# Attention, soft mixture of experts and a wide output layer: where the first two pairs' normalised values are computed, who issues the first loads of k, and another order of the attention's events

## The chip, the cores and the metric

One core of a Trainium2 chip runs the whole kernel as one program. The metric is the device time of one execution in microseconds (us). Engines are named as in the profile: PE (TensorE), DVE (VectorE), ACT (ScalarE), POOL (GpSimd) and SP (SyncE, which here only issues DMAs).

## The reference

q, k and v have the shape 4 x 12 x 448 x 64 (batch, heads, positions, columns). What is computed, cut to its core:

```python
q_n, k_n = rmsnorm(q, g_q), rmsnorm(k, g_k)        # x / sqrt(mean(x*x) + 1e-6) * g
scores = q_n @ k_n.T / sqrt(64)
attn = exp(scores - max) ; attn /= sum             # per row
x = (attn @ v), heads side by side                 # 1792 x 768
logits = x @ phi                                   # 768 x 32: 8 experts of 4 slots
slot_input = softmax(logits, axis 0).T @ x
slot_out[e] = relu(slot_input[e] @ w1[e]) @ w2[e]  # 768 x 1024 and 1024 x 768, 8 of each
x = softmax(logits, axis 1) @ slot_out
h = x @ w_in                                       # 768 x 2048
out = (max(h, 0) + alpha * min(h, 0)) @ w_out      # 2048 x 768
```

## The kernel before

**Tiles and stages.** The 48 heads are worked on as 24 pairs of two heads; two pairs that follow each other are a group and are loaded together. Each pair has 7 chunks of up to 128 rows (three per head and one that takes the rest of both heads). After the attention a soft mixture of experts follows (its statistics are gathered per batch, that is every six pairs), then eight experts whose weights stream in through eleven buffers of 1.5 MB, then the output layer. Seven of the eleven buffers lie where the attention's tiles were: two open when the last pair has been transposed and the event `cn` has come (`close_norm`), two at `cs` (the last scores), three at `ce` (the last products with v).

**The chain of a pair.** The loads of q and k (`load_to`, L599 to L612) bring a group into the tile qk. For each pair ACT squares it (sqr, L641; there is one buffer, `NSQ = 1`, L398) and DVE sums the squares into u (L643). For each group ACT and DVE turn u into the scale factors y (`norm_rs`, L653 to L663). `split_mul` (L668) makes the normalised values nf with three products: k times G, where G is the product of the two gains (L1151), then k times y, and q times y. There is one buffer nf (`"NNF": 1`). ACT casts nf to 16 bits (the high parts, L690), and `split_lo` (L692) subtracts them from nf to get the low parts (L697); both parts go into the tile sp. PE transposes sp (L710), ACT copies the result to the operands q and k (L717), and SP copies parts of these into the helpers qB and kB (L719, L721) and doubles q (L726).

The score rows are shifted by a coarse row maximum: PE computes the coarse scores (psr, L760), DVE reduces each to a maximum in the tile m (L769), PE turns m (L731), ACT copies it to mr (L737), and SP moves mr into a row of qB (L738). Then the scores proper are two matmuls a chunk, of k and q and of kB and qB (L778). ACT takes their exponential, once in 16 bits and once in 32 (L792 to L799), DVE or POOL subtract one from the other (L810), and PE multiplies with v (L827, L837). DVE also narrows the 64-bit weights w_in (win, L500 to L514) beside the attention.

**Who computes the products.** `T["PMUL"]` (L92) lists, for even and odd pairs, which of the three products (0 to 2) and two subtractions (3, 4) run on POOL. It lists all five for both, so POOL does all of them and DVE none.

**What sets the order.** The attention is written as 2374 small events (a product, a chunk's scores, one DMA piece, ...). Their order is the tuple `ORDER` (L232 to L350), a permutation worked out beforehand, and every engine executes its instructions in the order in which the events emit them; nothing is reordered later. Ahead of the events stand the constants, the loads of the first two groups of q and k, and the loads of the gains. All DMAs are issued by SP, one after the other.

Of the kernel before, what the change touches and what calls it, by code (L numbers as in the profile page):

```python
# [353 lines left out]
def fused_attention_softmoe_mlp(  # L354
# [15 lines left out]
    nc = tc.nc  # L370
    B, H, S, D = q.shape
# [6 lines left out]
    SM = 3 * P  # L378
# [213 lines left out]

    got = set()

    def load_to(g, src, dst, b0, t0):
        b, i = divmod(g * GP, NPAIR)
        s4 = src[b, 2 * i : 2 * (i + GP)].rearrange("(i h) t d -> h i t d", h=2)
        for h in range(2):
# [11 lines left out]
            ts = t0 + h if t0 == 6 else t0  # L610
# [414 lines left out]
    with tc.manual_schedule():  # L1025
# [120 lines left out]
        for _ in load_qk(0):  # L1146
            pass
# [403 lines left out]
```

## Time and profile before

| what | us |
|---|---|
| runs of the kernel before | 698.57, 696.68, 689.49 (median 696.68) |
| the profiled execution, its own time | 698.2 |
| its span, first to last instruction | 696.2 |

The span is what the rows below divide up; 2.0 us of the profiled execution lie around it. A group row gives the instructions of one line and tile with their mean duration, a stretch row the busy time of each engine in a piece of the span. In a timeline row the bracket gives how long the engine was idle before the instruction and who released it, as inferred.

### The profile page before, as it was taken

Reading aid. Unit: us, or ns where it says so; the run is one execution under the profiler, and the core shown is the slowest. Engines: PE = TensorE matmul, PEld = TensorE weight load, DVE = VectorE, ACT = ScalarE, POOL = GpSimd, SP = SyncE. Lnnn points to the kernel's source line nnn. Section 1 sums busy time; section 2 is a strip of 40 time slices with the busy share of each in tenths; the row PEclk is TensorE's granted clock in tenths of the full one; section 3 lists DMA queues with packets and bytes.
Section 4 is the critical chain, followed back from the end, with each engine's and each line's share of the span. In section 5 each row is a group of like instructions: output and inputs, shape, how many; then the busy total and the mean of one; then the engine's idle time right before and its main releaser. Section 6 shows DMA issues by size and latency. Waiting matters only on the chain.

```text
span 696.2 us, 14030 instructions
## 1 busy us (share of the span) xinstructions
PE 618.2 (89%) x5522; PEld 479.6 (69%) x5522; DVE 472.7 (68%) x967; ACT 364.5 (52%) x708; POOL 192.6 (28%) x200
## 2 busy tenths in 40 slices
PE   0799898898889999998998657899999999999997
PEld 0367665576656766775543213787899999999997
DVE  5788997899999999864311042999975545454541
ACT  2799996898898997772111121766531111111110
POOL 5976665466647654321101000000000000000000
PEclk9889999999999999998899979999999999999999
DMA  5477666644735622759799999250020101010101
GB/s 138 109 209 197 174 161 190 178 118 115 191 93 154 180 50 61 211 164 399 313 422 425 425 423 425 107 182 1 1 91 0 47 1 46 1 45 1 47 1 45
DMA packets 65425, 106.90 MB, mean 154 GB/s; under 512 B 34632, under 2 KB 51536, under 8 KB 61008
## 3 DMA queue, kind: packets, MB, share of 16 engines
q1 hardware_dynamic: 65360, 106.01, 45.6%
q8 instruction: 43, 0.70, 0.4%
q14 instruction: 22, 0.18, 0.1%
HBM read 92.18 MB, written 5.51 MB: 140 GB/s over the span
## 4 chain that ended last, share of the span: by engine, by line
PE 50%; DVE 23%; DMA 12%; ACT 8%; issue 3%; SPq 2%; POOL 2%; ACTq 0%; DVEq 0%; POOLq 0%
PE psa L1461 9%; PE psa L1460 9%; PE psa L1459 9%; DMA unit<-in_moe_w_dram 8%; DVE m L769 4%; PE psn L778 4%; PE psv L837 3%; PE psv L827 3%; PE psa L1285 2%; DVE e L810 2%; PE psr L760 2%; DVE wf L510 1%; ACT e L794 1%; PE psa L1314 1%; PE pst L1416 1%
## 5 line engine op out<-in xcount | busy, mean ns | idle before, releaser
L1459 PE MATMUL psa<-whi,gh 128*128 128x384 f32 (+1 forms) x448 | 152.7, 341 | 0.0
L1460 PE MATMUL psa<-wlo,gh 128*128 128x384 f32 (+1 forms) x448 | 151.8, 339 | 0.0
L1461 PE MATMUL psa<-whi,gl 128*128 128x384 f32 (+1 forms) x448 | 151.4, 338 | 0.0
L769 DVE TENSOR_REDUCE m<-psr 128x1 f16<-128x448 f32 x168 | 97.2, 615 | 5.9 <-PE psr L760 5.4
L1428 ACT CAST gh<-t 128x512 fp32r<-128x512 f32 x40 | 24.9, 622 | 123.0 <-DVE t L1425 122.5
L1461 PEld LDWEIGHTS psa<-whi,gl 128*128 128x128 f32 x448 | 84.7, 189 | 3.0 <-DVE gl L1408 0.2
L1460 PEld LDWEIGHTS psa<-wlo,gh 128*128 128x128 f32 x448 | 84.7, 189 | 2.8
L837 PE MATMUL psv<-vH,e 128*128 128x65 f16 (+1 forms) x1152 | 85.7, 195 | 1.0 <-DVE e L810 0.9
L1459 PEld LDWEIGHTS psa<-whi,gh 128*128 128x128 f32 x448 | 84.7, 189 | 2.6
L837 PEld LDWEIGHTS <-e 128*128 128x128 f16 (+1 forms) x1728 | 80.8, 106 | 1.5 <-DVE e L810 1.2
L1422 DVE TENSOR_SCALAR t<-pst,alpha_t 128x256 f32<-128x256 f32 x80 | 34.9, 476 | 61.9 <-PE pst L1416 61.9
L810 POOL TENSOR_TENSOR e<-ef,e 128x448 f16<-128x448 f32 x48 | 53.7, 1119 | 83.1 <-ACT ef L799 65.4
L827 PEld LDWEIGHTS psv<-vR,e 128*128 128x128 f32 (+1 forms) x384 | 59.6, 178 | 22.9 <-issue 10.9
L837 PE MATMUL psv<-vL,e 128*128 128x64 f16 (+1 forms) x576 | 73.7, 193 | 0.1
L794 ACT ACTIVATE e<-psn 128x448 f16<-128x448 f32 x120 | 65.1, 542 | 14.2 <-PE psn L778 11.1
L778 PE MATMUL psn<-q,k 128*128 128x448 f16 (+1 forms) x192 | 62.5, 368 | 11.0 <-DVE e L810 4.9
L827 PE MATMUL psv<-vR,e 128*128 128x65 f32 (+1 forms) x384 | 69.9, 264 | 1.9 <-DVE X L865 0.7
L760 PE MATMUL psr<-k,q 128*128 128x448 f16 (+1 forms) x192 | 58.8, 378 | 6.8 <-DVE m L769 4.0
L778 PE MATMUL psn<-qB,kB 67*128 67x448 f16 (+1 forms) x192 | 62.2, 364 | 2.8 <-DMA vR<-in_v_dram 2.8
L697 POOL TENSOR_TENSOR sp<-nf,sp 128x448 f16<-128x448 f32 x48 | 51.2, 1076 | 13.9 <-ACT sp L690 11.0
L810 DVE TENSOR_TENSOR e<-psn,e 128x448 f16<-128x448 f32 x72 | 44.2, 616 | 9.3 <-ACT psn L799 8.8
L710 PE MATMUL pst<-ident,sp 128*128 128x128 f16 x336 | 28.4, 233 | 19.2 <-POOL sp L697 19.0
(164 smaller groups left out, 1077.4 us busy)
## 6 DMA issues: line engine op xcount, KB each, us to landing
unit<-in_moe_w_dram SPq DMA_DIRECT2D x26, 1536.0 KB
unit<-in_moe_w_in_dram SPq DMA_DIRECT2D x24, 512.0 KB
rawo<-in_moe_w_out_dram SPq DMA_DIRECT2D x8, 1536.0 KB
unit<-in_moe_w_dram SPq DMA_DIRECT2D x36, 256.0 KB
out_dram<-osb SPq DMA_DIRECT2D x14, 384.0 KB
qk<-in_q_dram SPq DMA_DIRECT2D x24, 192.0 KB
qk<-in_k_dram SPq DMA_DIRECT2D x24, 192.0 KB
vR<-in_v_dram SPq DMA_DIRECT2D x48, 96.0 KB
```

Source lines behind the costliest of these rows:

```text
L697: eng.tensor_tensor(out=d["sp"][:, a, :, D:], in0=d["nf"][:, a], in1=d["sp"][:, a, :, 0:D], op=ALU.subtract)
L760: nc.tensor.matmul(pn[o0:o1, :S], d["q"][:, c0 : c0 + o1 - o0], d["k"][:, h * S : (h + 1) * S], start=True, stop=True)
L769: nc.vector.tensor_reduce(out=d["m"][:, c : c + 1], in_=d.pop(("pn", c))[:, :S], axis=AX.X, op=ALU.max)
L778: nc.tensor.matmul(pe[o0:o1, :S], lhs[:, c0 : c0 + o1 - o0], rhs[:, h * S : (h + 1) * S], start=st_, stop=not st_,)
L794: nc.scalar.activation(e2[:, 0], pe[:, :S], AF.Exp, scale=0.125)
L810: eng.tensor_tensor(out=e2[:, 1], in0=ef, in1=e2[:, 0], op=ALU.subtract)
L827: nc.tensor.matmul(pv[o0:o1, slot, :], d["e", c][:, qs], d["vv"][:, sl], start=(j == 0), stop=False,)
L837: nc.tensor.matmul(pv[o0:o1, slot, 0:wd], d["e", c][:, w // 2, qs], (vl if w == 1 else vh)[:, sl, 0:wd], start=(j == 0 and w == 0), stop=( ...
L1422: nc.vector.tensor_scalar(out=t0[:, cs], in0=ph[:, cs], scalar1=0.0, scalar2=alpha_t[:, f // 2, i : i + 1], op0=ALU.min, op1=ALU.mult)
L1459: nc.tensor.matmul(a, gh[f][:, ms], hi[:, hs], start=(f == 0 and not (packed and m % 2 == 1 and hf == 0)), stop=False)
L1460: nc.tensor.matmul(a, gh[f][:, ms], lo[:, hs], start=False, stop=False)
L1461: nc.tensor.matmul(a, gl[f][:, ms], hi[:, hs], start=False, stop=(f == KF - 1 and not (packed and m % 2 == 0 and hf == 1)))
```

## The change

Three things are changed. For pairs 0 and 1 the three products and two subtractions run on DVE instead of POOL. The four loads of k for the first group are issued by ACT instead of SP, and ACT's table load is placed behind them. The 2374 events of the attention are permuted anew.

```diff
 ORDER = (
-    1775, 968, 992, 1076, 920, 969, 993, 1016, 932, 1028, 1040, 1052, 1064, 1100, 1148, 1124, 921, 1796, 970, 994,
...
-    def load_to(g, src, dst, b0, t0):
+    def load_to(g, src, dst, b0, t0, eng=nc.sync):
...
-                    nc.sync.dma_start(
+                    eng.dma_start(
...
-            nc.sync.dma_start(dst[h * D : h * D + D, :, ts, :], s4[h, :, SM:S].rearrange("i p d -> p i d"))
+            eng.dma_start(dst[h * D : h * D + D, :, ts, :], s4[h, :, SM:S].rearrange("i p d -> p i d"))
...
         yield from load_to(g, q, qk[:, 0], 4, 3)
-        yield from load_to(g, k, qk[:, 1], 4, 3)
+        yield from load_to(g, k, qk[:, 1], 4, 3, nc.sync if g else nc.scalar)
...
-        eng = nc.gpsimd if w in T["PMUL"][n % 2] else nc.vector
+        eng = nc.gpsimd if n > 1 and w in T["PMUL"][n % 2] else nc.vector
...
-        eng = nc.gpsimd if 3 + a in T["PMUL"][n % 2] else nc.vector
+        eng = nc.gpsimd if n > 1 and 3 + a in T["PMUL"][n % 2] else nc.vector
...
-        nc.scalar.preload_act_table_set("natural_log_exp_and_others")
         for _ in load_qk(0):
             pass
+        nc.scalar.preload_act_table_set("natural_log_exp_and_others")
```

What the order does to the engines' lists is shown at three places. First ACT at the start, before (two squares for the first group, the y steps, the casts of pair 0, two squares for the next group, the copies of pair 0's transposes):

```order
L1145 ACT_TABLE_LOAD
L641 ACTIVATE sqr<-qk 128x896 x2
L653 ACTIVATE y<-u,eps 128x28
L654 ACTIVATE y<-y 128x28
L690 CAST sp<-nf 128x7x64
L641 ACTIVATE sqr<-qk 128x896
L690 CAST sp<-nf 128x7x64
L641 ACTIVATE sqr<-qk 128x896
L717 COPY q<-pst_230 128x896
L717 COPY k<-pst_257 128x896
L690 CAST sp<-nf 128x7x64
```

and in the changed kernel:

```order
L605 DMA qk<-in_k_dram 128x2x192
L611 DMA qk<-in_k_dram 64x2x64
L605 DMA qk<-in_k_dram 128x2x192
L611 DMA qk<-in_k_dram 64x2x64
L1147 ACT_TABLE_LOAD
L641 ACTIVATE sqr<-qk 128x896 x2
L653 ACTIVATE y<-u,eps 128x28
L654 ACTIVATE y<-y 128x28
L690 CAST sp<-nf 128x7x64 x2
L641 ACTIVATE sqr<-qk 128x896
L717 COPY q<-pst_236 128x896
L641 ACTIVATE sqr<-qk 128x896
```

The copy of k follows right behind. The second square of the next group stood ahead of both copies and now stands between them.

DVE at the same place, from its last constant on, before:

```order
L587 MEMSET X_134 128x128
L643 TENSOR_REDUCE u<-sqr 128x2x7 x2
L656 TENSOR_SCALAR u<-u 128x28
L659 TENSOR_TENSOR t<-y 128x28
L661 TENSOR_TENSOR t<-t,u 128x28
L663 SCALAR_TENSOR_TENSOR y<-t,y 128x28
L643 TENSOR_REDUCE u<-sqr 128x2x7 x2
L769 TENSOR_REDUCE m<-psr 128x1 x6
```

and in the changed kernel, from the last step of y on:

```order
L663 SCALAR_TENSOR_TENSOR y<-t,y 128x28
L684 TENSOR_TENSOR nf<-nf,y 128x448
L684 TENSOR_TENSOR nf<-qk,y 128x448
L697 TENSOR_TENSOR sp<-nf,sp 128x7x64 x2
L684 TENSOR_TENSOR nf<-qk,G 128x448
L684 TENSOR_TENSOR nf<-qk,y 128x448
L643 TENSOR_REDUCE u<-sqr 128x2x7
L684 TENSOR_TENSOR nf<-nf,y 128x448
L643 TENSOR_REDUCE u<-sqr 128x2x7
L769 TENSOR_REDUCE m<-psr 128x1
```

The products and subtractions of pair 0 stand ahead of the sums of the next group, and two products of pair 1 do too. (The first product of pair 0 stands between the two sums of the first group; the two subtractions of pair 1 come behind the first row maximum.)

SP around the maxima of pair 7 (mr into qB1; unit is an expert's or w_in's weight buffer, the numbers are those of tiles), before:

```order
L719 DMA kB2_119<-k_1664 64x896
L488 DMA unit_1493<-in_moe2_w_in_dram 128x1024
L726 DMA q_1438<-q_1438 64x896
L479 DMA unit_1760<-in_moe_w1_dram 128x512 x3
L738 DMA qB1_116<-mr_1778 1x7x128
L479 DMA unit_1760<-in_moe_w1_dram 128x512
L601 DMA vR0_122<-in_v_dram 128x3x64 x2
```

and in the changed kernel:

```order
L726 DMA q_1414<-q_1414 64x896
L488 DMA unit_1544<-in_moe2_w_in_dram 128x1024
L719 DMA kB2_119<-k_1712 64x896
L738 DMA qB1_116<-mr_1772 1x7x128
L479 DMA unit_1775<-in_moe_w1_dram 128x512 x2
L601 DMA vR0_122<-in_v_dram 128x3x64 x2
```

The three pieces of expert weights that stood ahead of the maxima now stand behind them. Of the three events that open weight buffers, `cn` stood behind the first four score chunks of pair 22 and now stands ahead of the first; `cs` stood behind the last products with v and now stands behind the last score chunk.

## Rows read from the trace of the kernel before

**Rows 1.** The page, busy us, share of the span and instructions of an engine.

```profile
PE 618.2 (89%) x5522; PEld 479.6 (69%) x5522; DVE 472.7 (68%) x967; ACT 364.5 (52%) x708; POOL 192.6 (28%) x200
```

**Rows 2.** Stretches: the attention proper and its last part (first line: the columns).

```profile
core 0: us, PE busy (x) PEld busy (x) DVE busy (x) ACT busy (x) POOL busy (x), PEclk, DMA share, GB/s
40.00:280.00 240.00, 217.39 (x2734) 159.78 (x2732) 225.37 (x463) 213.77 (x435) 145.19 (x136) 0.98 0.55 148
280.00:320.00 40.00, 39.40 (x573) 30.30 (x571) 27.84 (x70) 28.13 (x62) 11.15 (x11) 1.00 0.67 216
```

**Rows 3.** Stretches after the attention, columns as in rows 2.

```profile
336.00:338.00 2.00, 2.00 (x18) 0.55 (x12) 1.86 (x6) 0.00 (x0) 1.01 (x1) 0.87 0.02 4
...
400.00:420.00 20.00, 11.85 (x79) 3.68 (x80) 8.64 (x16) 4.51 (x6) 0.00 (x0) 0.74 1.01 423
...
480.00:696.00 216.00, 212.12 (x1229) 206.19 (x1227) 119.61 (x215) 48.80 (x84) 0.00 (x0) 1.00 0.07 26
```

**Rows 4.** Timeline of the start, and the experts' first matmul: start us, us, engine, line.

```profile
0.73 1.28 ACT L1145 ACT_TABLE_LOAD   x1 [0.73 <-PEq L1535]
...
3.32 0.60 SPq L605 DMA_DIRECT2D qk<-in_k_dram  x1
...
8.11 0.95 ACT L641 ACTIVATE sqr<-qk 128x896 f32<-128x896 f32 x1 [6.10 <-DMA gqk<-in_g_q_dram]
...
10.46 1.09 DVE L643 TENSOR_REDUCE u<-sqr 128x14 f32<-128x896 f32 x1
...
14.73 0.19 DVE L663 SCALAR_TENSOR_TENSOR y<-t,y 128x28 f32<-128x28 f32 x1
...
15.00 0.93 POOL L684 TENSOR_TENSOR nf<-qk,y 128x448 f32<-128x448 f32 x1 [2.16 <-DVE y L663]
...
16.79 2.16 POOL L697 TENSOR_TENSOR sp<-nf,sp 128x448 f16<-128x448 f32 x2
...
18.54 0.95 ACT L641 ACTIVATE sqr<-qk 128x896 f32<-128x896 f32 x1 [0.70 <-DVE u L643]
...
19.00 0.93 PE L710 MATMUL pst<-ident,sp 128*128 128x128 f16 x7 [0.20 <-POOL sp L697]
...
20.18 0.91 ACT L717 COPY k<-pst 128x896 f16<-128x896 f16 x1
...
21.91 2.02 POOL L697 TENSOR_TENSOR sp<-nf,sp 128x448 f16<-128x448 f32 x2
...
334.67 1.94 PE L1285 MATMUL psa<-unit,slT 128*32 128x512 f32 x8
```

**Rows 5.** Groups of DVE by shape: busy us, mean ns of one.

```profile
L1429 DVE TENSOR_TENSOR gl<-t,gh 128x512 fp32r<-128x512 f32 x40 | 27.5, 687 | 3.0 <-ACT gh L1428 2.3
...
L1252 DVE TENSOR_TENSOR wlo<-wf,whi 128x768 fp32r<-128x768 f32 x16 | 15.2, 952 | 1.0 <-ACT whi L1250 0.9
```

**Rows 6.** Tile vL on DVE (ns min/median/max), and DVE beside POOL at 42.7 us.

```profile
L747 DVE SCALAR_TENSOR_TENSOR vL<-vR,vH x24: 677/686/1510, 38.6 to 311.5; 128x512 f16<-128x512 f32 x24
...
42.73 1.31 DVE L747 SCALAR_TENSOR_TENSOR vL<-vR,vH 128x512 f16<-128x512 f32 x1
...
43.45 1.48 POOL L810 TENSOR_TENSOR e<-ef,e 128x448 f16<-128x448 f32 x1
```

**Rows 7.** Timeline around the scores of pair 7.

```profile
104.57 0.80 SPq L738 DMA_DIRECT2D qB<-mr  x1
...
111.11 0.46 PE L778 MATMUL psn<-qB,kB 67*128 67x448 f16 x1 [2.79 <-DMA vR<-in_v_dram]
...
113.77 0.63 DVE L769 TENSOR_REDUCE m<-psr 128x1 f16<-128x448 f32 x1 [1.52 <-PE psr L760]
...
116.17 0.62 DVE L810 TENSOR_TENSOR e<-psn,e 128x448 f16<-128x448 f32 x1 [1.77 <-ACT psn L799]
```

**Rows 8.** Stretches around the scores of pair 7, columns as in rows 2.

```profile
107.00:111.00 4.00, 0.90 (x11) 0.47 (x8) 3.85 (x9) 2.99 (x6) 4.00 (x4) 1.00 1.04 313
111.00:115.00 4.00, 3.89 (x39) 3.65 (x40) 1.88 (x4) 1.00 (x2) 2.52 (x4) 0.57 0.76 223
```

More of the change, by code (lines that the diff above doesn't have):

```diff
@@ L604, in load_to @@
             else:
-                nc.sync.dma_start(
+                eng.dma_start(
                     dst[:, :, b0 * h : b0 * h + 3, :].rearrange("p i r d -> p i (r d)"),
```

233 rows, old and new, of the table ORDER are left out of this document.

## The prediction

> **What bounds the kernel now.** I read the page's busy times first, then a table by stretches, then the stretches in which an engine that should be full is not. The page has PE at 89% and DVE at 68% of the span [rows 1], which are averages over stages with different limits. By stretches it looks otherwise. From 40 to 280 us, the attention proper, DVE is busy 225.37 of 240 us and PE 217.39, so DVE is the tighter one and idles only 14.6 us; from 280 to 320 us PE is, with 39.40 of 40 [rows 2]. After that the experts' weights bound: in 336 to 338 us the DMA queues move 4 GB/s, because every weight buffer is full and PE has only begun to use them, and from about 339 us on they move some 423 GB/s, to 420 us and beyond; in the last 216 us PE is busy 212.12 [rows 3]. The experts' first matmul starts at 334.67 [rows 4]. So the end of the attention is passed on one to one to the start of the experts, from there to the stream of weights and from there to the end, as long as the buffers are full when PE comes to them. The margin is that pause, some 4 us: an attention that is more than 4 us shorter would begin to wait for the weights instead. The code after the attention is not changed. What counts is when the attention begins at full pace, and how much DVE and PE idle in it.
>
> **The change part by part.** The loads of k for the first group go from SP's queue to ACT's. SP issued the first of them at 3.32 us, each takes 0.60 us of the queue, and the first square began at 8.11 us [rows 4]. Four issues, 2.6 us in all, now run beside SP's. But what a square feeds is the sum on DVE, and DVE is at its constants until that sum starts, without a wait, at 10.46 us, 1.4 us after the square had ended [rows 4]. DVE's list up to there is the same after the change, so earlier data only wait longer for DVE. ACT's table load, 1.28 us [rows 4], now stands behind the four issues and would end near 4.6 us, before any square. Should the constants end sooner than I think, at most the 2.4 us between 8.11 and 10.46 could be won; should k land later on the second queue, the square has 1.4 us to spare before anything is lost. I take 0.
>
> The second part is the ten products and subtractions of pairs 0 and 1. On POOL a product takes 0.93 us and two subtractions 2.16 [rows 4]. The trace has no such operation on DVE, so I bound it by two neighbours with both inputs in SBUF: 0.687 us for 512 columns and 0.952 for 768 [rows 5], which lie on a line that gives an estimate of 0.62 for 448 columns, and about 0.55 from one start to the next since they overlap by some 0.07. The scale factors y are ready at 14.92 us as before (the last step starts at 14.73) [rows 4]. Then, on DVE: product of k 14.95 to 15.57, of q to 16.1; ACT casts k 15.6 to 16.15 and q to 16.7; subtractions to 16.7 and 17.35. The transposes of q then run from 17.4 and those of k from 18.3 to 19.2, where the second set had begun at 19.00 and taken 0.93 [rows 4]: 0.7 us won. It is lost again on ACT. Before the change the second square of the next group stood ahead of both copies and ran at 18.54; the copy of k began at 20.18 [rows 4]. Now that square stands between the copy of q and the copy of k, and it needs the one square buffer that the sum on DVE frees, and this sum now stands behind two products of pair 1. That gives: products 17.35 to 18.45, sum to 19.5, square to 20.45, copy of k 20.45 to 21.35, against 20.18 to 21.09. For pair 1 the last subtraction comes out at 24.4 us by the same reckoning, against POOL's two that started at 21.91 and took 2.02 [rows 4]. The ten operations, 5.5 us of DVE, fall into time in which DVE waited. Sum of the front: 0, with 1.5 us to either side, as DVE's list from 21 to 37 us has a dozen small waits that I can't settle.
>
> Here a rule speaks against the change. In the trace DVE's subtraction for vL, median 686 ns, took 1.31 us at 42.73, and POOL's subtraction that began at 43.45 took 1.48, the two side by side [rows 6]. The Trainium skill (SBUF — State Buffer, Who interferes with whom) says that a DVE instruction with two SBUF inputs and a GpSimd instruction that reads SBUF exclude each other for a whole instruction; the trace agrees, with those 1.31 and 1.48 us. All ten moved operations have two SBUF inputs. They would meet POOL only if POOL worked beside them, and its next product, of pair 2, needs the single buffer nf, which pair 1 frees with the last of the ten. So I charge nothing, and keep the collision as a rival.
>
> The third part is the new order of 2374 events, which moves rows on every engine through the attention. The largest idle place of the old order is at 107 to 116 us. SP issues the row maxima of pair 7 (mr into qB) at 104.57, right behind three pieces of expert weights; the scores that need it start at 111.11 after PE had idled 2.79 us, and DVE then waits 1.52 us at 113.77 and 1.77 at 116.17 [rows 7]. In the same 8 us the DMA queues are full (1.04), PE is busy 0.90 of 4 us and then works at a mean granted clock of 0.57, that is some 3.4 of those 4 us at the 1.2 GHz level [rows 8]. In the new order the three pieces stand behind that small transfer, and some 57 matmuls still stand between; I count DVE's 3.3 us as won. Bounds: 0, if one piece of w_in (512 KB) that still stands ahead delays it as much, and 3.3. For the rest of the order I find no place that decides. DVE's other waits between 40 and 280 us, 11.3 us, are many small ones; the new order leaves somewhat more DVE work between most producers and their readers, but also puts pair 6's maxima closer to its scores. I take 0, between -6 and +6: half of those 11.3 us either way.
>
> Sum on the profiled execution: 0 + 0 - 3.3 = -3.3, from 698.2 to 694.9 us. That execution lies 1.5 us above the median of the three runs, 696.68, and within their spread; the forecast of a median is 696.7 - 3.3 = 693.4 us.
>
> **The rivals.**
> - The front pays too: the 0.7 us won at the transposes survives and pair 1 follows, some 2 us. For it: five POOL operations of 0.93 to 1.08 us give way to 0.62. Against it: the square ahead of the copy of k. Then 691.4 us.
> - The gaps close all over, DVE regains most of its 14.6 us. For it: the longer distances. Against it: the weights' pause of 4 us caps what the attention can give back, unless the weights start earlier as well, and the close of the normalisation's buffers does move forward past pair 22's scores. Some 10 us: 686.7 us.
> - Slower: the wait at pair 7 is moved and not removed. In the new order the maxima of pair 6 follow a 512 KB piece of w_in and a 192 KB load of q on SP, and only some 47 matmuls (54 before) stand between turn and use, an estimate of 3.8 us of PE work, where pair 7's transfer needed 6.5 us from issue to use, 104.57 to 111.11 [rows 7]. From the point where such a transfer takes longer than that work, PE idles; priced by pair 7, DVE's 3.3 us and 1.7 for half of the 3.4 us at the lower clock, 5 us. With nothing won at pair 7: 701.7 us.
> - Slower by collisions: if POOL ran beside all ten operations, each would lose 0.62 (1.31 - 0.69), 6.2 us on the front: 699.6 us with pair 7 won.
> - The change doesn't do what it says for k: the loads go out earlier and nothing starts earlier. That is part of my forecast, not against it.
>
> **How the numbers follow.** My forecast 0.50 (693.4, own range 689 to 698); front pays 0.15; gaps close 0.12; waits moved 0.18; collisions 0.05. The range 685 to 702 holds the rivals' centres, with the run-to-run spread of 689.49 to 698.57 in mind, and leaves about 2 in 10 outside. 2%, about what a measurement of this kernel can tell from no change, is 13.9 us. Faster by that, below 682.7, would take nearly all of DVE's idle time: 0.04. Slower, above 710.6, would take three places like pair 7's: 0.05. Within: 0.91.
>
> **What would show it right or wrong.** In the new profile DVE's first sum should still start near 10.4 us, the copy of k of pair 0 near 21.3, the first row maximum's matmul near 21.4, and the ten operations take about 0.62 us each. DVE's wait behind pair 7's scores should be gone, and DVE busy some 228 of 240 us between 40 and 280. The experts' first matmul should move from 334.67 to about 331.4 and the end with it. I am wrong on the front if that matmul at 21.4 comes below 20, wrong on the order if a wait of over 1.5 us on qB stands at another pair, and wrong on the bound if the attention ends earlier and the total does not.

## The result, and the profile after

| | us |
|---|---|
| the kernel before, median of 4 runs | 697.62 (689.49 to 698.87) |
| the changed kernel, median of 4 runs | 703.64 (700.92 to 706.51) |
| ratio | 1.0118, 95% interval 1.0073 to 1.0162 |
| the profiled execution of the changed kernel, its span | 703.6, 701.8 |

The changed kernel is slower by 1.2%, some 8 us (5 to 11): less than 2%, but not zero, and 1.6 us above the upper end of the predicted range. Ratios here compare fast runs alone; runs over 1.5% above the fastest of their kernel are left out as slow, which in e8 are four of twelve, its profiled one among them.

The stretches show where to look. The columns are those of [rows 2], and the first two lines answer to it, the third to the pause in [rows 3].

```profile
40.00:280.00 240.00, 217.41 (x2774) 160.34 (x2773) 227.08 (x461) 214.91 (x437) 144.65 (x136) 0.99 0.55 149
280.00:320.00 40.00, 35.32 (x456) 26.55 (x456) 27.22 (x69) 26.99 (x59) 10.50 (x11) 0.96 0.57 174
...
340.00:342.00 2.00, 2.00 (x15) 0.46 (x11) 1.90 (x5) 0.00 (x0) 1.15 (x1) 0.50 0.03 4
```

From 40 to 280 us DVE is busier than before, 227.08 against 225.37 us, and the forecast of "some 228" holds. But in 280 to 320 us, which PE filled to 39.40 of 40 us, PE is now busy 35.32. The pause of the weight stream, 4 GB/s, has moved from 336 to 340 us: it is still there, so the experts' weights still come early enough and the end of the attention still decides.

The front is the part that came as forecast. The rows of the timeline answer to [rows 4]: DVE's first sum, the last step of y, the first two products of pair 0 behind it and its two subtractions; ACT's copy of k; PE's first row maximum.

```profile
10.45 1.09 DVE L643 TENSOR_REDUCE u<-sqr 128x14 f32<-128x896 f32 x1
...
14.73 0.19 DVE L663 SCALAR_TENSOR_TENSOR y<-t,y 128x28 f32<-128x28 f32 x1
14.95 0.62 DVE L684 TENSOR_TENSOR nf<-nf,y 128x448 f32<-128x448 f32 x1
15.50 0.62 DVE L684 TENSOR_TENSOR nf<-qk,y 128x448 f32<-128x448 f32 x1
16.21 1.16 DVE L697 TENSOR_TENSOR sp<-nf,sp 128x448 f16<-128x448 f32 x2
...
20.45 0.89 ACT L717 COPY k<-pst 128x896 f16<-128x896 f16 x1
...
21.39 1.28 PE L760 MATMUL psr<-k,q 128*128 128x448 f16 x3 [2.29 <-ACT k L717]
```

A product takes 0.62 us on DVE (estimated 0.62), the copy of k runs from 20.45 to 21.34 (forecast 20.45 to 21.35), the matmul starts at 21.39 (forecast 21.4).

Two waits are new. The first stands at the first scores of pair 3. SP issues three pieces of w_in at 57.56, then the doubling of pair 3's q (L726) and its maxima (L738); PE reaches the scores and waits, and DVE waits behind PE.

```profile
57.56 1.57 SPq L488 DMA_DIRECT2D unit<-in_moe_w_in_dram  x3
59.23 0.59 SPq L726 DMA_DIRECT2D q<-q  x1
60.18 0.81 SPq L738 DMA_DIRECT2D qB<-mr  x1
...
67.84 0.36 PE L778 MATMUL psn<-q,k 128*128 128x448 f16 x1 [2.07 <-DMA q<-q]
...
69.32 0.63 DVE L769 TENSOR_REDUCE m<-psr 128x1 f16<-128x448 f32 x1 [2.46 <-PE psr L760]
...
72.84 0.63 DVE L769 TENSOR_REDUCE m<-psr 128x1 f16<-128x448 f32 x1 [1.05 <-PE psr L760]
```

The doubling needed 8.6 us from issue to use. In the kernel before, two pieces stand ahead of it, and pair 3's scores begin without a wait:

```profile
55.41 1.07 SPq L488 DMA_DIRECT2D unit<-in_moe_w_in_dram  x2
56.57 0.52 SPq L726 DMA_DIRECT2D q<-q  x1
...
63.70 0.35 PE L778 MATMUL psn<-q,k 128*128 128x448 f16 x1
```

The second stands at the first scores of pair 23. ACT has copied pair 23's maxima at 302.75, but SP is still issuing ten weight pieces, 0.6 us each.

```profile
299.94 6.05 SPq L479 DMA_DIRECT2D unit<-in_moe_w_dram  x10
...
302.49 0.26 ACT L737 CAST mr<-pst 7x128 f16<-7x128 f32 x1
...
306.08 0.78 SPq L738 DMA_DIRECT2D qB<-mr  x1
...
310.47 0.35 PE L778 MATMUL psn<-qB,kB 67*128 67x448 f16 x1 [2.76 <-DMA qB<-mr]
...
312.38 0.62 DVE L810 TENSOR_TENSOR e<-psn,e 128x448 f16<-128x448 f32 x1 [3.42 <-ACT psn L799]
```

So the 1.8 KB of maxima lose 3.3 us before they are issued, and 4.4 us more pass until the matmul. In the kernel before they were copied by 302.95 and issued at once, and the pieces followed:

```profile
302.70 0.25 ACT L737 CAST mr<-pst 7x128 f16<-7x128 f32 x1
...
302.98 0.77 SPq L738 DMA_DIRECT2D qB<-mr  x1
303.85 6.94 SPq L479 DMA_DIRECT2D unit<-in_moe_w_dram  x12
```

What does this is the place of one event: `cn` opens two weight buffers, twelve pieces in all, and in the new order ten events that issue a piece stand between it and the copy of pair 23's maxima.

What the two waits cost on PE and on its clock is in the same view by 4 us:

```profile
66.00:70.00 4.00, 2.16 (x20) 1.69 (x21) 1.54 (x3) 2.01 (x4) 3.92 (x5) 0.94 0.61 146
70.00:74.00 4.00, 4.00 (x50) 3.51 (x49) 2.87 (x5) 3.02 (x7) 0.01 (x1) 0.63 0.31 74
...
306.00:310.00 4.00, 1.65 (x17) 1.25 (x18) 2.50 (x6) 1.83 (x4) 1.03 (x1) 1.00 1.00 369
310.00:314.00 4.00, 3.53 (x40) 3.11 (x41) 1.25 (x2) 2.78 (x6) 0.00 (x0) 0.73 0.21 78
```

PE stands half of 66 to 70 us and more than half of 306 to 310, and runs at a mean granted clock of 0.63 and 0.73 after each. Pair 7's wait [rows 7] is gone: its maxima are issued at 110.93, and its first scores follow each other without a wait.

```profile
114.97 0.35 PE L778 MATMUL psn<-q,k 128*128 128x448 f16 x1
...
115.16 0.35 PE L778 MATMUL psn<-qB,kB 67*128 67x448 f16 x1
```

The experts' first matmul comes at 338.52 instead of 334.67, 3.85 us later, while the span grew by 5.6. Most of the other 1.7 us arises at once behind it, before and after:

```profile
334.67 4.53 PE L1285 MATMUL psa<-unit,slT 128*32 128x512 f32 x24
...
338.52 5.62 PE L1285 MATMUL psa<-unit,slT 128*32 128x512 f32 x24
```

The same 24 matmuls took 1.1 us longer. PE's stretch at the 1.2 GHz level ended in 336 to 338 us before (mean 0.87 [rows 3]); now 340 to 342 us still lie wholly in it (0.50 in the third line of the first view), so it covers more of the experts' first matmuls. The last 0.7 us were not followed.

### The profile page after: what moved, and what is told of

Read it like the earlier page. It is cut to its first block, busy times and chain, and to the rows that moved or that the text cites. A ratio compares the mean times of both kernels' runs of the same rounds, so it can differ in the third digit from the quotient of the medians.

```text
span 701.8 us, 14038 instructions
## 1 busy us (share of the span) xinstructions
PE 616.1 (88%) x5522; PEld 478.7 (68%) x5522; DVE 479.3 (68%) x977; ACT 365.3 (52%) x708; POOL 182.6 (26%) x190
## 4 chain that ended last, share of the span: by engine, by line
PE 44%; DVE 28%; DMA 16%; ACT 6%; issue 3%; POOL 2%; SPq 0%; DVEq 0%; ACTq 0%; POOLq 0%
DMA unit<-in_moe_w_dram 11%; PE psa L1461 9%; PE psa L1459 9%; PE psa L1460 9%; DVE m L769 6%; PE psn L778 3%; DVE e L810 3%; PE psv L837 2%; PE psv L827 2%; DVE u L643 2%; DVE wf L510 1%; DVE win L510 1%; PE pst L1416 1%; PE psa L1285 1%; DVE wf L514 1%
## 5 line engine op out<-in xcount | busy, mean ns | idle before, releaser
L697 POOL TENSOR_TENSOR sp<-nf,sp 128x448 f16<-128x448 f32 x44 | 47.5, 1088 | 11.9 <-ACT sp L690 11.8
L1285 PE MATMUL psa<-unit,slT 128*32 128x512 f32 x192 | 33.6, 673 | 13.4 <-DMA unit<-in_moe_w_dram 13.3
```

The lines of the kernel that those rows point to most:

```text
L697: eng.tensor_tensor(out=d["sp"][:, a, :, D:], in0=d["nf"][:, a], in1=d["sp"][:, a, :, 0:D], op=ALU.subtract)
L1285: nc.tensor.matmul(ph[hf][32 * g : 32 * g + 32, :], slT[:, t, :], wu[:, t % 3, hf * 512 : (hf + 1) * 512], start=(hf, g) not in seen, stop ...
```

## The experiments

Theory A: the loss is the two waits, small transfers that the next scores need and that stand behind weight pieces. The rival: DVE's added work, 479.3 us busy instead of 472.7 [rows 1], is paid in an attention that DVE bounds. Each ratio is to the kernel before on the same chip; its median was 694.4 to 696.3 us in these comparisons.

A table read from DVE's and PE's timelines goes with them: the start, in us, of the step that takes a pair's sums (z, L852), the experts' first matmul, and the span. It is one profiled execution of each, and single executions of one kernel differ by some us too.

| | pair 0 | pair 2 | pair 4 | pair 21 | pair 23 | experts | span |
|---|---|---|---|---|---|---|---|
| before | 48.87 | 70.83 | 92.53 | 305.41 | 319.73 | 334.67 | 696.2 |
| after | 50.21 | 74.31 | 99.41 | 304.95 | 323.75 | 338.52 | 701.8 |
| e1 cn late | 50.79 | 75.62 | 100.75 | 306.83 | 321.29 | 335.63 | 698.2 |
| f1 pieces behind | 50.84 | 71.62 | 96.75 | 302.97 | 321.64 | 336.42 | 704.0 |
| e5 both | 50.09 | 70.79 | 95.90 | 301.72 | 316.18 | 330.51 | 693.2 |
| e2 before, pieces first | 48.80 | 70.78 | 92.48 | 300.74 | 321.30 | 336.07 | 700.4 |
| e3 new code, old order | 54.44 | 76.41 | 98.10 | 309.30 | 323.62 | 337.48 | 699.8 |
| e6 new front, old rest | 49.70 | 71.67 | 93.36 | 304.64 | 318.97 | 333.04 | 696.0 |
| f3 old front, new rest | 50.19 | 70.92 | 95.81 | 301.13 | 315.59 | 329.57 | 691.6 |

In the diffs of orders, events stand by their names (`mm3 22`: scores of chunk 3 of pair 22; `pf`: next weight piece; `turnedm`: copy and transfer of the maxima; `twin`: the doubling of q).

**e1: the wait at pair 23 taken away from the changed kernel.**

```diff
 rm4 23
-cn
 xT 20
...
 turnedm 23
+cn
 mm3 22
```

> The changed kernel with one event moved: the normalisation's buffers close (cn) behind the row maxima of pair 23, so that the first ten pieces of the weights that use these buffers stand behind that small transfer on SP and not ahead of it. Theory A (the loss is at pair 23: its maxima were ready at 302.75, issued at 306.08 behind ten pieces, and PE waited 2.76 us at 310.47): the wait goes, the experts' first matmul comes at about 335 instead of 338.5, the total falls by 3.5 to 5.5 us, from 703.6 to 698 to 700. Theory B (the loss is spread over the middle of the new order, DVE having lost 4.5 us between 40 and 80): no change, 703 to 704.

Measured: 1.0081 (1.0056 to 1.0107). SP now issues the maxima first:

```profile
304.65 0.77 SPq L738 DMA_DIRECT2D qB<-mr  x1
305.51 10.75 SPq L479 DMA_DIRECT2D unit<-in_moe_w_dram  x13
```

From pair 21 to pair 23 it takes 14.5 us, as before (14.3), against 18.8 in the changed kernel: 4.3 us for this place. In the time only 0.37 points show, 2.6 us, less than the 3.5 to 5.5 expected and within the intervals of the two ratios; in the profiled execution the wait at pair 3 happened to be longer (PE 2.73 us, after: 2.07). The rest of the loss is elsewhere.

**e2: the same wait put into the kernel before.**

```diff
 rm6 23
+cn
+pf
...
 turnm 23
...
-cn
...
 turnedm 23
...
-pf
```

> The kernel before with ten pieces of weights and the close of the normalisation's buffers put directly ahead of the row maxima of pair 23, and nothing else. Theory A: a PE wait of some 3 us appears at the scores of pair 23, the experts start 3 to 4 us later, the total rises by 3.5 to 5.5 us to about 701 to 703. Theory B: no change, about 697.

Measured: 1.0136 (1.0099 to 1.0173). The close and the ten pieces (ten `pf`) stand ahead, PE's wait appears, and nothing else was changed:

```profile
296.85 5.87 SPq L479 DMA_DIRECT2D unit<-in_moe_w_dram  x10
...
303.03 0.78 SPq L738 DMA_DIRECT2D qB<-mr  x1
...
306.73 0.56 PE L778 MATMUL psn<-qB,kB 67*128 67x448 f16 x1 [3.36 <-DMA qB<-mr]
```

From pair 21 to 23: 20.6 us, 6.2 more than before. The place alone makes the old kernel as slow as the changed one; the time rose by 9.4 us where 3.5 to 5.5 were expected, and what makes up the part beyond the 6.2 was not followed. Until the ten pieces at 296.85 this kernel is the one before, instruction for instruction, and yet pair 20 comes at 291.29 instead of 295.97. Of these 4.7 us 3.1 are there by pair 6 (118.08 against 121.22): at pair 7's scores, where the profile of before has its wait of 2.79 us, this execution waits for no DMA.

**e3 and e4: the new code in the old order, the old code in the new order.**

```diff
 ORDER = (
-    1775, 920, 932, 2171, 968, 992, 969, 1796, 1797, 1076, 993, 1016, 1028, 1040, 921, 933, 1052, 1064, 1124, 1100,
+    1775, 968, 992, 1076, 920, 969, 993, 1016, 932, 1028, 1040, 1052, 1064, 1100, 1148, 1124, 921, 1796, 970, 994,
```

for e3, and the reverse in the kernel before for e4.

> The kernel before with the products and subtractions of pairs 0 and 1 on DVE and the first loads of k issued by ACT, in the old order of events. Theory A (the front is worth nothing either way): 697 within 1.5 us. Rival (DVE is the tighter engine and pays for its ten more operations, 5.5 us): about 702. Rival (the front pays): 694 to 695.

> The kernel before with the new order of events alone: products on POOL, all loads by SP. Theory A (the order, at pair 23, makes the whole difference): as the full change, 702 to 705. Rival (the code makes the difference and the order was fitted to it): about 697, or, if the new order without the code it was made for starves at the front, above 706.

Measured: e3 1.0137 (1.0111 to 1.0163), e4 1.0184 (1.0147 to 1.0221). The code alone, which the forecast had at 0, costs as much as the whole change; the order alone more; and the two do not add up. In e3 DVE's timeline shows why:

```profile
15.52 0.62 DVE L684 TENSOR_TENSOR nf<-nf,y 128x448 f32<-128x448 f32 x1
17.09 1.09 DVE L643 TENSOR_REDUCE u<-sqr 128x14 f32<-128x896 f32 x1 [0.94 <-ACT sqr L641]
19.19 1.09 DVE L643 TENSOR_REDUCE u<-sqr 128x14 f32<-128x896 f32 x1 [1.02 <-ACT sqr L641]
20.19 1.15 DVE L697 TENSOR_TENSOR sp<-nf,sp 128x448 f16<-128x448 f32 x2
...
20.95 1.65 PE L710 MATMUL pst<-ident,sp 128*128 128x128 f16 x14 [20.95 <-DVE sp L697]
```

The old order has the sums of the next group ahead of pair 0's subtractions. On POOL these passed them; on DVE they stand behind two sums that wait for squares. The first transposes begin at 20.95 us instead of some 17.9, and pair 0's sums come 5.6 us late (54.44 against 48.80 in e2). That is also the 5.5 us that e3's rival charged for ten more operations on DVE; e6 below, with the same operations in another order, tells the two apart. In e4 the products are on POOL and the new order has its two waits as well (PE waits 2.93 us for q at 70.10, and 1.89 for the maxima at 313.70). Besides, it is behind the changed kernel from the front on (pair 0 at 51.59 against 50.21), which is what the last part of its expectation, above 706 us, describes. That the new code improves the new order by 0.66 points, from 1.0184 to 1.0118, just clear of the intervals, says that the two belong together.

**e7 and e8: e3 taken apart.** The old order with only the loads of k moved (e7: both products' lines as before), and with only the products moved (e8).

```diff
-        eng = nc.gpsimd if n > 1 and w in T["PMUL"][n % 2] else nc.vector
+        eng = nc.gpsimd if w in T["PMUL"][n % 2] else nc.vector
...
-        yield from load_to(g, k, qk[:, 1], 4, 3, nc.sync if g else nc.scalar)
+        yield from load_to(g, k, qk[:, 1], 4, 3)
```

The first two lines (and the same at the subtractions) are e7's, the last two e8's, both against e3.

> The old order and the old engines for the products, with only the first group's loads of k issued by ScalarE. Theory A (the loads cost nothing, VectorE's constants hide them): first sum of squares at 10.4 to 10.5 us, ratio 1.000 (0.997 to 1.003). Theory B (the loads carry part of the 8 us that the new code costs in the old order): ratio over 1.004.

> The old order with only the products and subtractions of pairs 0 and 1 on VectorE, all loads issued by SyncE. Theory A (in the old order VectorE's queue has the sums of the next group ahead of the products, so that pair 0's first transposes come at about 21 us instead of 17.9, and each later product pushes the row maxima): like the new code in the old order, ratio 1.011 to 1.015, pair 0's sums of weights at 54 to 55 us. Theory B (the products are hidden as forecast and the loads are what costs): ratio 1.000 to 1.004.

Measured: e7 1.0012 (0.9978 to 1.0046): the loads cost and bring nothing that an interval of 2.4 us to each side shows, as forecast. e8 1.0048 (1.0009 to 1.0088), with pair 0's sums at 54.60 us: the place of the loss is e3's, but the time lies between the two expectations and its interval is wide. Where the products lose in the old order rests on the two traces, not on this ratio. And e7's 0.12 and e8's 0.48 points do not make up e3's 1.37: the rest, some 0.8 points, is beyond the intervals and stays open.

**e5 and f1: the pieces behind pair 3's maxima.** e5 has it besides e1's edit, f1 alone in the changed kernel. Five events are moved; three of them issue a piece.

```diff
 cv
-pf
 rm0 4
...
 turnedm 3
+pf
```

> The changed kernel with the event cn behind pair 23's copy of the maxima (as in the run before) and, besides, the five weight pieces that stand between chunk 1 of pair 2's scores and pair 3's copy of the maxima moved behind that copy, so that pair 3's twin and maxima are issued ahead of them. Theory A (small transfers that the next scores need stand behind weight pieces, and this is paid one to one): TensorE's wait of 2.07 us at 67.8 and VectorE's of 2.46 us at 69.3 go, the experts' first matmul comes at 332.5 to 333.5 instead of 335.6, the ratio to before falls from 1.0081 to about 1.0045 (1.002 to 1.007). Theory B (VectorE's 6.6 us of added work are the cost and the wait is only where its slack happens to lie): the wait goes, but the experts' first matmul stays within 0.7 us of 335.6 and the ratio at 1.007 to 1.010.

> The changed kernel with only the five weight pieces behind pair 3's copy of the maxima; cn stays where the change put it. Theory A (each wait of the next scores on a transfer behind weight pieces is paid by itself, and the two add up): the wait at 67.8 goes, the one at 310 on the maxima of pair 23 stays at 2 to 3.5 us, the experts' first matmul comes at 333 to 334 instead of 338.5, ratio about 1.004 (1.001 to 1.007). Rival (the two waits share one cause, or the later one swallows what the earlier gives back): ratio 1.008 to 1.012.

Measured: e5 1.0003 (0.9971 to 1.0035), f1 1.0078 (1.0050 to 1.0106). In e5 SP's timeline reads

```profile
57.50 0.54 SPq L726 DMA_DIRECT2D q<-q  x1
60.07 0.81 SPq L738 DMA_DIRECT2D qB<-mr  x1
60.93 3.04 SPq L488 DMA_DIRECT2D unit<-in_moe_w_in_dram  x3
```

and PE is busy in both places:

```profile
66.00:70.00 4.00, 3.67 (x57) 3.03 (x55) 3.73 (x6) 4.00 (x10) 3.92 (x4) 1.00 0.94 254
...
306.00:310.00 4.00, 3.94 (x72) 3.49 (x70) 1.25 (x2) 2.70 (x7) 0.10 (x1) 1.00 0.96 314
```

With both waits gone the changed kernel is level with the one before: the experts' first matmul at 330.51, 8.0 us earlier than after, and 1.15 points of the ratio, also 8 us (4.2 to 11.8). DVE is busy 479.5 us in it, as in after: its added work is all there, and the loss is gone, so the rival falls. e5 went further than expected (1.0045). f1 shows pair 3's repair by itself: 0.40 points, 2.8 us, and the wait at pair 23 stays (2.65 us of PE at 308.37). Its time is nearer to what the rival in its expectation gave, and its matmul came at 336.42, not 333 to 334. Singly the repairs give 2.6 and 2.8 us, which intervals of some 3.6 us to each side do not tell from nothing; on top of the other each is clear of it, 0.78 points at pair 3 (e5 against e1) and 0.75 at pair 23 (e5 against f1), 5 us each with some 3 to each side. Together they give 8.0. Whether they help each other or merely add up stays open.

**e6: the new front, the old rest.** The changed code, the first 191 events of the new order, then the others in the old one.

```diff
 rm5 2
 lo5 0
-av0 0
-av3 0
+loq 4
+rmm6 2
```

> The changed kernel's code with the first 191 events of the new order (up to the first output matmul of pair 0, some 43 us) and then the remaining events in the old order. Theory A (the new front order fits the new code; what costs is the rest of the new order): pair 0's sums of weights at 49.5 to 51 us against 48.8 in the old kernel, no waits over 2 us later, the ratio about 1.003 (0.999 to 1.006), that is 6 us faster than the new code in the old order all through (1.0137). Theory B (6.6 us more of VectorE's work in an attention that VectorE bounds are paid wherever they stand): ratio 1.008 to 1.011.

Measured: 1.0024 (0.9997 to 1.0051), with pair 0's sums at 49.70. The new front with its products on DVE costs between nothing and 3.5 us; against the 1.37% of the same code in the old order it is nearly free. The rival had 1.008 at the least.

**f2: the forecast's own gain, alone in the kernel before.**

```diff
 twin 7
 cv
-pf
 cv
 mm3 6
-pf
-pf
...
 turnedm 7
+pf
+pf
+pf
```

> The kernel before with the three weight pieces ahead of pair 7's maxima moved behind their copy: the one gain that the forecast saw, made alone. Theory A (the wait of 2.79 us at 111 that the forecast removed is one of a wait that differs from run to run: 2.79, 0, 1.22 and 2.82 us in four traces with this order): the wait is gone in the trace, and the ratio is 0.9975 (0.995 to 1.000). Rival (the pieces aren't what the transfer waits for, but the loads of the values behind it): the wait stays between 1 and 3 us, ratio 1.000.

Measured: 0.9993 (0.9959 to 1.0026). No gain that the interval tells from nothing (2.8 us won to 1.8 lost), and a wait is still there:

```profile
109.98 0.36 PE L778 MATMUL psn<-q,k 128*128 128x448 f16 x1 [1.54 <-DMA q<-q]
```

It now falls on pair 7's doubling, which two pieces of w_in still precede. Neither expectation holds whole, and the ratio does not choose between them: the wait on the maxima went, as theory A had it, and another of half its size stands in its place.

**f3 and f4: the old front, the repaired new rest.** The code of the kernel before (products on POOL), the first 191 (f3) or 290 (f4) events of the old order, then the new order with both repairs. At the seam of f3:

```diff
 lo5 0
 av0 0
-lo6 0
-mulk 5
+cv
+f1
```

> The kernel before's code with the first 191 events of the old order and then the rest of the new order with both repairs (cn late, the five pieces behind pair 3's maxima): the counterpart of the run that joined the new front to the old rest. Theory A (the new order's rest is as good as the old one once its two waits are gone, and the old front is 1.3 us ahead of the new one at pair 0's sums of weights, 48.8 against 50.1 us): experts' first matmul at 329 to 330, ratio 0.998 (0.995 to 1.001). Rival (the rest of the new order is made for the new front): new waits of over 2 us in it, ratio over 1.003.

> As the run with the old front and the new rest, but with the first 290 events of the old order (to the first scores of pair 2, past pair 3's twin), so that pair 0's output phase keeps its old place too. Theory A (what pair 0 gains is passed on): pair 0's sums of weights at 48 to 49 us instead of 50.2, the experts' first matmul at 328 to 329.3 instead of 329.57, ratio 0.9955 (0.993 to 0.998). Rival (the lead of 1.4 us is taken back where the two orders join, as VectorE's work is the same): first matmul within 0.5 us of 329.57 and ratio 0.997 to 1.000.

Measured: f3 0.9974 (0.9949 to 1.0000), f4 0.9990 (0.9960 to 1.0020). f3 has the lowest ratio of all, with an upper end at 1, and no clear gain over e5; pair 0's sums came at 50.19, no earlier than in e5, so if it gains, not from the front as theory A had it. f4 has them at 48.02, and the rival of its expectation is right: at 54.54 DVE waits 1.84 us for ACT, by pair 4 the lead is 0.3 us, and the first matmul is at 329.63 like f3's.

## Why the prediction was wrong

The bound was right. The experts' first matmul passes the attention's end on to the end of the run: from that matmul to the end it takes 361.5 us before, 363.3 after, and 361.7 to 364.5 in all other runs but f1. "One to one" left out up to 2.9 us. (f1's profiled execution took 367.6 and lies 3.7 us above the median of that kernel; what it lost there was not followed.)

The front was right: the loads at 0 (e7), the ten operations at 0 with 1.5 us to either side (e6: 1.7 us, interval 0 to 3.5; pair 0's sums 1.3 us later), its times to a tenth of a us, but for pair 1's last subtraction, which ended at 24.02 instead of 24.4. What the forecast did not say is that this 0 belongs to the new front's order alone: in the old one it is 5.6 us at pair 0. The rule on SBUF, charged at nothing, was not put to the test, as POOL's first product starts at 24.15 us, behind the last of the ten.

The term of -3.3 us for pair 7 was mis-sized. The wait is gone after the change, but its price was read from one execution. With the same events and the same DMAs around it, PE waited there 2.79 us in the profile of before, 1.22 in e7 and for no DMA in e2; freeing the transfer in the kernel before gave 0.5 us (f2, 2.8 won to 1.8 lost), with a wait of 1.54 us in its place. For a median the term was nearer to 0 than to 3.3. The forecast also took the wait for one on the maxima without saying why: the bracket in [rows 7] names a load of v, which SP issued behind them.

The step that failed is "For the rest of the order I find no place that decides ... I take 0, between -6 and +6". There were two places, at pair 3 and at pair 23, and they are worth some 8 us together (e5 against after, 4.2 to 11.8), where the forecast had 0 and 6 at the most. That bound was made from DVE's idle time in the old trace, and a wait that the new order makes has no row there. The argument weighed the work between producers and readers on the engines; what decided was the queue between them, SP's, and the transfers ahead on it. At pair 3 four pieces of w_in (512 KB each in the page's list of issues) were issued in the 3.4 us ahead of the doubling, where the kernel before had two in 1.2 us. At pair 23 ten pieces of 256 KB stand ahead, and PE's wait of 2.76 us on qB there is the very sign that the forecast had named for being wrong on the order.

The rival that came true is "the wait at pair 7 is moved and not removed": its mechanism, its sign, and its price as far as the interval tells (5 us; found 8, 4.2 to 11.8). Its place was wrong. At pair 6 the trace after shows no such wait. The forecast compared pair 6 with pair 7 and did not go on to the other pairs. And the event `cn` it did notice, but as a reason for the opposite rival: weights that start earlier were to lift the cap on a gain. They started earlier (299.94 against 303.85), and in the way.

The Trainium skill (DMA: Bandwidth & Descriptors, Two DMAs through the same engine are not ordered) says that within one queue of a DMA engine descriptors start in the order in which they stand. The trace after is in keeping with it and shows no more: 1.8 KB issued at 306.08 were used at 310.47, while the DMA queues moved 369 GB/s at a share of 1.00; which of them started first stands in no row. The Trainium skill says on the same page that the time to issue a DMA is usually small beside the transfer (Issuing engines are not separate DMA queues). For one piece that holds here, 0.6 us of issue against 4.3 us to landing in the page's list of issues; but ten of them held SP for 6.05 us, and 3.3 us of that were the maxima's delay.

## What to carry to other kernels

When an order is permuted, go through the queue that issues the DMAs pair by pair: for each small transfer that the next matmuls need, note how many bytes and how many issues were put ahead of it, and how much work of the waiting engine lies between. An event that frees a buffer for a prefetch is an event on that queue, and counts with everything that it lets loose. A wait that one execution shows becomes a term of a sum only when a second one shows it.

## What was not expected of the hardware

The same sequence of issues gave PE waits on DMAs of 2.79, 1.22 and 0 us at pair 7, so what waits behind a row of weight pieces can differ by up to 2.8 us from one execution to the next. It carries on: e2 is 3.1 us ahead of the profiled execution of before at pair 6's sums, 4.7 us at pair 20's, with the same instructions up to there. (In e7, with 1.22 us, the lead over before is gone again by pair 13: 211.21 against 211.22.)

A wait of PE also costs behind itself: the mean granted clock was 0.63 and 0.73 in the 4 us after the two waits, against 1.00 in the same two stretches of e5, where PE had not waited:

```profile
70.00:74.00 4.00, 4.00 (x53) 3.00 (x50) 3.88 (x12) 3.97 (x10) 1.39 (x2) 1.00 0.42 97
...
310.00:314.00 4.00, 4.00 (x58) 2.65 (x56) 1.90 (x6) 2.49 (x6) 1.96 (x2) 1.00 0.98 323
```
